# Gated linear attention and a token/channel mixer: keys of batch 0 through SP's queue, factor rows read with a step

## The chip, the cores and the metric

The kernel runs on one core of a Trainium2 chip. The metric is the device time of one execution in microseconds. The engines are named as in the profile: PE (TensorE, matmuls; PEld its weight loads), DVE (VectorE), ACT (ScalarE), POOL (GpSimd) and SP (SyncE, which only issues DMAs and waits). [...]

## The reference

Inputs are q, k, v and f_logit of 4 batches, 8 heads, 768 steps and 48 channels, and the four weights of a mixer, all float32.

```python
f = 1.0 / (1.0 + np.exp(-f_logit))
for t in range(S):
    state = f[:, :, t, :, None] * state + np.einsum('bhd,bhe->bhde', k[:, :, t], v[:, :, t])
    y[:, :, t] = np.einsum('bhd,bhde->bhe', q[:, :, t], state)
x = y.transpose(0, 2, 1, 3).reshape(B, S, H * D)          # 4 x 768 x 384
h = np.maximum(x.transpose(0, 2, 1) @ w_tok1, 0.0) @ w_tok2
u = x + h.transpose(0, 2, 1)
out = u + np.maximum(u @ w_ch1, 0.0) @ w_ch2
```

## The kernel before, in words

Each batch is cut into 6 chunks of 128 steps, with the steps on the partitions and 8 x 48 = 384 channels along the row. For a chunk, `gates` makes the logarithm of 1/f on ACT (an exponential and a logarithm, L479 and L480) and, on DVE or POOL, the low part `Llo` that the bfloat16 upper half of it leaves out (L485). `sums_and_turns` sums the logarithms along the chunk by matmuls with a triangle (L552 to L555; the last chunk of batch 0 in float32, L543), and ACT takes from PSUM the factors G and Gi = exp of minus and plus the sum (L565, L567). DVE scales q by G and k by Gi (L586); PE transposes both (L603), and DVE or ACT copies the transposes back (`qkT`, L459 and L461). `attention` multiplies them (L504), DVE masks the product (`AmT`, L640), and `rest` adds the part of earlier chunks (L671) and of this chunk (L678) to the output y, while DVE carries the state along (L649 to L654) and ACT or POOL copies it to bfloat16 (`state_bd`).

The state needs one factor a channel, that of the chunk's last step. In batch 0 it comes of small matmuls (L552) and one small exponential (`glast`, L570). In later batches ACT takes the exponential of the sums' last 32 partitions into `ends` (L574), and SP moves partition 127 of it, turned, into `glast` by a DMA (L580). `ends` lies as (parity, channel, head pair), so that this DMA reads it in a row; the sums lie as (head pair, parity, channel).

`mixer` then does the two token matmuls (L708, L724), turns u (L765), and does the two channel matmuls (L783 with a ReLU into `zT`, L802 with the final sum on DVE, L808, and the store by SP, L812). The chunks of the next batch's attention are laid between the matmuls of the mixer before it.

The order of all work is made when the program is built. Every operation is given to a planner with its engines, a rank, what it needs and makes, and an assumed duration; the planner fills each engine's queue by the earliest start, with ranks breaking ties. The table `SHIFTS` overrides rank and adds a lag for some 560 operations by number; `LATE` adds to the assumed landing of some loads. On the chip each engine runs its queue in that order and waits with semaphores. Where PE would stand idle at the start, the planner puts matmuls on a constant tile (`steady`, L849).

Loads of batch 0 go one chunk at a time. f comes by SP in float32; k, q and v come by POOL, converted to bfloat16 into `qk_sb` and `v_sb`. SP's load of f for chunk c + 2 waits for a small memset on POOL (`mark`, L382) that stands behind POOL's issue of q for chunk c, so that SP's loads are spaced by POOL's issues. Weights and later batches follow in POOL's queue. `x_nat` holds the float32 y of a batch, in three buffers; buffer 2 is first used by batch 2.

Of the kernel before, what the change touches and what calls it, by code (L numbers as in the profile page):

```python
# [86 lines left out]
)  # L87
KEPT = 3
SPLIT = 5
# [211 lines left out]
def kernel(  # L301
# [109 lines left out]
    def once(engine, fn, make, own):  # L411
        add(engine, -5.0, fn, make=make, kind=("fix", own, own))

    add(POOL, -20.0, lambda: None, kind=("load", 600, 600, 0))
    load("f", 0, 0, SP)
    load("f", 0, 1, SP)
    load("kq", 0, 0)
    mark(2)
# [7 lines left out]
    for c in range(1, NCH):  # L426
        load("kq", 0, c)
        if c + 2 < NCH:
            mark(c + 2)
            load("f", 0, c + 2, SP)  # L430
# [452 lines left out]
```

## Time and profile before

| | |
|---|---|
| median of 3 runs | 181.43 us (181.07 to 182.17) |
| profiled execution, its own time | 180.95 us |
| its span | 179.1 us |
| PE, busy | 166.3 us (93%), 11.6 us of it fillers (L849) |
| DVE, ACT, POOL, busy | 128.1, 125.8, 100.7 us |
| granted clock | 1.0 |
| SP's loads of f in batch 0, issue to landing | 4.1 us, median of 6 |
| POOL's loads of k, q and v, issue to landing | 5.3, 5.5, 5.3 us, medians of 24 |

The span is the time from the first to the last instruction of the program; the execution's own time is 1.85 us longer. Busy times of one engine overlap those of the others, so they don't add up; what counts in a stage is which engine the others wait for there.

### The profile page before, as it was taken

How to read it: one execution, taken by the hardware profiler on the slowest of the kernel's cores; microseconds unless marked ns; L12 is line 12 of the kernel's file. 1: busy time of each engine (PE TensorE's matmuls, PEld its weight loads, DVE VectorE, ACT ScalarE, POOL GpSimd, SP SyncE). 2: the span in 40 equal slices, each digit the busy share in tenths (PEclk: the TensorE clock that was granted, in tenths of full speed). 3: DMA queues.
4: the chain of work that ended last, by engine and by line, in shares of the span. 5: the costliest groups of instructions: out<-in, count | busy, mean ns of one | idle time of the engine just before them, and what ended most of it. 6: DMA issues, size and time to landing. Idle time of an engine off the chain costs nothing.

```text
span 179.1 us, 4283 instructions
## 1 busy us (share of the span) xinstructions
PE 166.3 (93%) x1649; PEld 104.8 (59%) x1653; DVE 128.1 (72%) x286; ACT 125.8 (70%) x273; POOL 100.7 (56%) x136
## 2 busy tenths in 40 slices
PE   6888898899998999799899999999999999999991
PEld 2445565556665665465566656676666666656660
DVE  6469886996878999887949987699674666501331
ACT  4678894699798786999899689976844432695000
POOL 7999569696599969977992996521102211000000
PEclk9999999999999999999999999999999999999999
DMA  7999999999999999999997999944812011200132
GB/s 105 127 165 157 148 149 182 211 142 203 183 167 152 213 247 91 199 91 89 113 161 40 89 201 137 189 91 108 93 31 89 3 44 47 90 0 0 73 117 77
DMA packets 97796, 21.54 MB, mean 120 GB/s; under 512 B 90512, under 2 KB 96912, under 8 KB 97776
## 3 DMA queue, kind: packets, MB, share of 16 engines
q0 software_dynamic: 79440, 13.77, 96.1%
q1 hardware_dynamic: 18336, 7.51, 19.0%
q8 instruction: 13, 0.21, 0.6%
q14 instruction: 7, 0.06, 0.1%
HBM read 25.17 MB, written 4.72 MB: 167 GB/s over the span
## 4 chain that ended last, share of the span: by engine, by line
PE 46%; ACT 11%; DVE 3%; issue 1%
PE ps L802 19%; PE ps L783 15%; ACT ends L574 3%; PE ps L724 2%; PE ps L708 2%; ACT zT L468 2%; PE ps L765 1%; ACT u_bf L459 1%; ACT GG L567 1%; PE ps L504 1%; PE ps L678 1%; PE ps L671 1%; PE ps L603 1%; ACT f_sb L479 1%; ACT state_bd L459 1%
## 5 line engine op out<-in xcount | busy, mean ns | idle before, releaser
L783 PE MATMUL ps<-uT,w_ch 128*128 128x384 bf16 x288 | 51.9, 326 | 1.2 <-ACT zT L468 0.7
L802 PE MATMUL ps<-w_ch,zT 128*128 128x384 bf16 (+2 forms) x300 | 52.4, 320 | 0.0
L468 ACT ACTIVATE zT<-ps 128x384 bf16<-128x384 f32 x70 | 33.2, 491 | 12.2 <-PE ps L783 9.9
L783 PEld LDWEIGHTS <-w_ch 128*128 128x128 bf16 x288 | 27.2, 98 | 18.1 <-issue 1.6
L802 PEld LDWEIGHTS <-zT 128*128 128x128 bf16 x300 | 27.7, 98 | 16.6
L640 DVE TENSOR_TENSOR AmT<-ps,tri_bf 128x512 bf16<-128x512 f32 x46 | 29.9, 683 | 3.3 <-PE ps L504 3.1
L401 POOL DMA_DIRECT2D v_sb<-in_v_dram x24 | 22.4, 931 | 4.7 <-DMA w_ch<-in_moe_w_ch_dram 4.7
L808 DVE TENSOR_TENSOR x_nat<-x_nat,ps 128x384 f32<-128x384 f32 (+2 forms) x25 | 13.3, 535 | 15.4 <-PE ps L802 15.3
L401 POOL DMA_DIRECT2D qk_sb<-in_k_dram x24 | 22.7, 944 | 0.8 <-POOLq L867 0.8
L401 POOL DMA_DIRECT2D qk_sb<-in_q_dram x24 | 22.6, 944 | 0.0
L470 DVE TENSOR_SCALAR zT<-ps 128x384 bf16<-128x384 f32 x26 | 13.8, 551 | 8.7 <-PE ps L783 8.7
L586 DVE TENSOR_TENSOR qk<-qk_sb,GG 128x768 bf16<-128x768 bf16 (+1 forms) x30 | 14.9, 501 | 6.0 <-ACT GG L567 2.6
L463 POOL CAST state_bd<-state 48x192 bf16<-48x192 f32 x13 | 4.4, 342 | 21.8 <-DVE state L654 11.4
L401 POOL DMA_DIRECT2D f_sb<-in_f_logit_dram x18 | 16.5, 943 | 0.2
L479 ACT ACTIVATE f_sb<-f_sb 128x384 f32<-128x384 f32 x24 | 12.4, 517 | 4.9 <-DMA f_sb<-in_f_logit_dram 4.7
L603 PE MATMUL ps<-ident,qk 128*128 128x128 bf16 x144 | 11.4, 220 | 1.9 <-DVE qk L586 1.8
L849 PE MATMUL ps<-steady 128*128 128x512 bf16 x37 | 11.6, 433 | 1.6 <-DVE steady L433 1.5
L574 ACT ACTIVATE ends<-ps 32x384 f32<-32x384 f32 x15 | 12.7, 861 | 0.3
L459 ACT ACTIVATE state_bd<-state 48x192 bf16<-48x192 f32 x27 | 9.7, 360 | 4.2 <-DVE state L654 3.5
L565 ACT ACTIVATE GG<-ps 128x384 bf16<-128x384 f32 x24 | 11.6, 488 | 1.4 <-PE ps L555 1.1
L603 PEld LDWEIGHTS <-qk 128*128 128x128 bf16 x144 | 8.8, 98 | 5.8 <-DVE qk L586 4.2
L567 ACT ACTIVATE GG<-ps 128x384 bf16<-128x384 f32 x24 | 11.3, 493 | 0.5 <-PE ps L555 0.3
(75 smaller groups left out, 249.2 us busy)
## 6 DMA issues: line engine op xcount, KB each, us to landing
out_dram<-x_nat SPq DMA_DIRECT2D x23, 192.0 KB, 3.0
f_sb<-in_f_logit_dram POOLq DMA_DIRECT2D x18, 192.0 KB, 5.4
qk_sb<-in_k_dram POOLq DMA_DIRECT2D x24, 96.0 KB, 5.3
qk_sb<-in_q_dram POOLq DMA_DIRECT2D x24, 96.0 KB, 5.5
v_sb<-in_v_dram POOLq DMA_DIRECT2D x24, 96.0 KB, 5.3
f_sb<-in_f_logit_dram SPq DMA_DIRECT2D x6, 192.0 KB, 4.1
w_ch<-in_moe_w_ch_dram POOLq DMA_DIRECT2D x2, 576.0 KB, 8.6
w_ch<-in_moe_w_ch_dram POOLq DMA_DIRECT2D x1, 1152.0 KB, 10.2
```

Of the source, the lines that this page charges most:

```text
L401: lambda eng=eng, into=into, of=of: eng.dma_start(out=into, in_=of),
L459: nc.scalar.activation(out_, in_, AF.Copy, bias=0.0, scale=1.0)
L468: nc.scalar.activation(out_, in_, AF.Relu, bias=0.0, scale=1.0)
L470: nc.vector.tensor_scalar(out_, in_, 0.0, None, ALU.max)
L479: add(ACT, r, lambda: nc.scalar.activation(fb, fb, AF.Exp, bias=0.0, scale=-1.0), make=[key], kind=el)
L574: add(ACT, r, lambda: nc.scalar.activation(ends[g4][96:128, :, 0:D].rearrange("t par d hp -> t hp par d"), sview()[96:128].rearrange("t (h ...
L586: add(DVE, r, lambda n=n: nc.vector.tensor_tensor(qk[i4][:, n, :, 0:D], qk_sb[nb][:, n, :, c, :], GG[i][:, n], ALU.mult), need=[(x, nb, c) ...
L603: nc.tensor.transpose(to[:, o + hp, :], blk(src)[:, hp, :], ident)
L640: add(DVE, r, lambda half=half, made=made: nc.vector.tensor_tensor(half, made(), tb4, ALU.mult), need=["tri_bf"], make=[("AmT", i, p)], ba ...
L783: nc.tensor.matmul(banks[pm.at][:, 0:384], lhsT=w[:, kt, c0:c0 + 128], rhs=uT[:, th, :, kt, :], start=(kt == 0), stop=(kt == 2))
L802: nc.tensor.matmul(banks[pm.at][:, 0:n1 - n0], lhsT=zT[:, kt, tt * 128:(tt + 1) * 128], rhs=w_ch2[:, kt, n0:n1], start=(kt == 0), stop=(kt ...
L808: add(DVE, rank("ch2", tt), lambda un=un, pm=pm, n=n1 - n0: nc.vector.tensor_tensor(un, un, banks[pm.at][:, 0:n], ALU.add), make=[("x_nat" ...
```

## The change

- Keys of batch 0 no longer come by POOL. SP loads them in float32 into buffer 2 of `x_nat`, and DVE's scaling of k reads them from there, writing bfloat16 as before. Only k of batch 0 is concerned; q and v stay with POOL.
- The marks are no longer called. SP's queue now holds f and k of chunk 0, f and k of chunk 1, and so on, twelve loads in a row that wait for nothing. POOL's queue at the start holds q and v of each chunk in turn.
- The exponential into `ends` writes in a row and reads the sums with a step (one float32 of each of the four head pairs, 384 bytes apart); before, it read in a row and wrote with a step of 16 bytes.
- `SHIFTS` is another table and `LATE` is empty; the planner's assumed sizes of loads are others (800 for SP's, 650 for POOL's q and v of batch 0). The order of the queues differs throughout: 38 fillers on PE for 41, six state copies moved from ACT to POOL, four of `zT` from DVE to ACT. The number of PE's other matmuls is the same.

```diff
-LATE = {("f", 0, 1): 900, ("f", 0, 2): 200, ("f", 0, 3): 600, ("f", 0, 4): 700, ("f", 0, 5): 900,
...
+LATE = {}
...
+            if engine == SP and n == "k":
+                into = x_nat[2][:, c, :].rearrange("t (h d) -> t h d", d=D).unsqueeze(2)
...
-            size = 1050 if n == "f" else 760
+            size = 800 if engine == SP else 1050 if n == "f" else 650 if b == 0 else 760
...
-                kind=("load", 430 if engine == SP else 900,
+                kind=("load", 800 if engine == SP else 900,
...
     load("f", 0, 0, SP)
+    load("k", 0, 0, SP)
+    load("q", 0, 0)
     load("f", 0, 1, SP)
-    load("kq", 0, 0)
-    mark(2)
-    load("f", 0, 2, SP)
     load("v", 0, 0)
...
     for c in range(1, NCH):
-        load("kq", 0, c)
-        if c + 2 < NCH:
-            mark(c + 2)
-            load("f", 0, c + 2, SP)
+        load("k", 0, c, SP)
+        if c + 1 < NCH:
+            load("f", 0, c + 1, SP)
+        load("q", 0, c)
         load("v", 0, c)
...
-                ends[g4][96:128, :, 0:D].rearrange("t par d hp -> t hp par d"),
-                sview()[96:128].rearrange("t (hp par) d -> t hp par d", par=2), AF.Exp, bias=0.0, scale=-1.0),
+                ends[g4][96:128, :, 0:D],
+                sview()[96:128].rearrange("t (hp par) d -> t par d hp", par=2), AF.Exp, bias=0.0, scale=-1.0),
...
+        def raw(n):
+            if b == 0 and n == 1:
+                return x_nat[2][:, c, :].rearrange("t (h d) -> t h d", d=D)
+            return qk_sb[nb][:, n, :, c, :]
+
...
-                qk[i4][:, n, :, 0:D], qk_sb[nb][:, n, :, c, :], GG[i][:, n], ALU.mult),
+                qk[i4][:, n, :, 0:D], raw(n), GG[i][:, n], ALU.mult),
```

The listing of the changed program gives the start of DVE's queue, behind the first chunk's work: scaling of k of chunk 1, the two masks of chunk 0, scaling of q of chunk 1, the state of chunk 0, scaling of q and k of chunk 2, the two copies of chunk 1's transposes, and so on.

More of the change, by code (lines that the diff above doesn't have):

```diff
@@ L396, in load @@
             into = dst[i][:, :, cs, :]
+            if engine == SP and n == "k":
+                into = x_nat[2][:, c, :].rearrange("t (h d) -> t h d", d=D).unsqueeze(2)
             of = src[b].rearrange("h (c t) d -> t h c d", t=C)[:, :, cs, :]
             eng = nc.gpsimd if engine == POOL else nc.sync
-            size = 1050 if n == "f" else 760
+            size = 800 if engine == SP else 1050 if n == "f" else 650 if b == 0 else 760
             add(engine, 30.0 if b else 3.0 * c - (9.0 if engine == SP else 6.0),
                 lambda eng=eng, into=into, of=of: eng.dma_start(out=into, in_=of),
-                make=[(n, i, j) for j in range(cs.start, cs.stop)],
-                kind=("load", 430 if engine == SP else 900,
+                make=[(n, i, j) for j in range(cs.start, cs.stop)] + ([("x_nat", 2, c)] if engine == SP and n == "k" else []),
+                kind=("load", 800 if engine == SP else 900,
                       128 * H, size, 8000 if b else 20000, LATE.get((n, b, c), 0)))
@@ L586, in sums_and_turns @@
             add(DVE, r, lambda n=n: nc.vector.tensor_tensor(
-                qk[i4][:, n, :, 0:D], qk_sb[nb][:, n, :, c, :], GG[i][:, n], ALU.mult),
-                need=[(x, nb, c) for x in names] + [({"q": "G", "k": "Gi"}[x], i) for x in names],
-                make=[(x + "h", i4) for x in names], kind=("el", DM * len(names), False, 2))
+                qk[i4][:, n, :, 0:D], raw(n), GG[i][:, n], ALU.mult),
+                need=[(x, nb, c) for x in names] + ([("x_nat", 2, c)] if b == 0 and names == ["k"] else []) + [({"q": "G", "k": "Gi"}[x], i) for x in names],
+                make=[(x + "h", i4) for x in names], kind=("el", DM * len(names), False, 1 if b == 0 and names == ["k"] else 2))
         if b >= TURNED:
```

126 rows, old and new, of tables (LATE, SHIFTS) are left out of this document.

## The prediction

> **What bounds the kernel now.** I read the page's busy times and slices first, then the table of stages, then the chain of waits inside the stage where TensorE (PE) stands idle, and last the forms of instructions and the DMA packets at the start.
>
> ```profile
> PE 166.3 (93%) x1649; PEld 104.8 (59%) x1653; DVE 128.1 (72%) x286; ACT 125.8 (70%) x273; POOL 100.7 (56%) x136
> ```
>
> PE is the bound of the span (179.1 us; the profiled run took 180.95 us, so 1.85 us lie around it), but 11.6 us of its busy time are fillers of L849. Its real work, some 155 us, cannot shrink by this change: the listing of the new program has the same matmuls, with 38 fillers for 41. So time can come only from the start and from PE's idle stretches. The stages (columns: PE, PEld, DVE, ACT, POOL busy, clock, DMA) show one such stretch:
>
> ```profile
> 60.00:70.00 10.00, 10.00 (x131) 6.89 (x129) 9.88 (x22) 7.65 (x19) 8.08 (x11) 1.00 1.74 162
> 70.00:80.00 10.00, 8.31 (x71) 4.88 (x67) 9.17 (x21) 9.55 (x22) 8.74 (x11) 1.00 1.78 158
> 80.00:90.00 10.00, 8.83 (x96) 5.56 (x96) 8.12 (x17) 9.03 (x20) 8.87 (x11) 1.00 1.21 95
> 90.00:100.00 10.00, 9.74 (x108) 6.46 (x106) 7.50 (x14) 8.81 (x20) 6.43 (x8) 1.00 1.03 91
> 100.00:110.00 10.00, 9.70 (x117) 6.23 (x116) 8.61 (x19) 8.51 (x19) 10.00 (x13) 1.00 1.82 155
> ```
>
> From 70 to 110 us PE misses 1.69 + 1.17 + 0.26 + 0.30 = 3.4 us, while ACT is 85 to 95% busy. The chain of waits there runs along ACT (start, length, what):
>
> ```profile
> 72.96 1.56 ACT ends L574 x2
> ...
> 81.08 0.85 ACT ends L574
> ...
> 86.82 0.85 ACT ends L574
> ...
> 90.79 0.85 ACT ends L574
> ...
> 102.76 0.87 ACT ends L574
> ```
>
> Six of the fifteen factor rows stand on it. The forms say why they are dear:
>
> ```profile
> L574 ACT ACTIVATE ends<-ps 32x384 f32<-32x384 f32 x15 | 12.7, 861 | 0.3
> L565 ACT ACTIVATE GG<-ps 128x384 bf16<-128x384 f32 x24 | 11.6, 488 | 1.4 <-PE ps L555 1.1
> L586 DVE TENSOR_TENSOR qk<-qk_sb,GG 128x384 bf16<-128x384 bf16 x12 | 4.3, 362 | 2.3 <-ACT GG L565 1.4 <-DMA qk_sb<-in_q_dram 0.8
> L485 DVE TENSOR_TENSOR Llo<-f_sb 128x384 bf16<-128x384 f32 x6 | 3.3, 553 | 0.1
> ```
>
> The same 384 elements from PSUM cost 861 ns when written 16 bytes apart, 488 ns when written in a row. The start is bound by DMA packets and by DVE: from 15 to 25 us DVE is busy for 4.40 and 4.60 of each 5 us. Packets by queue, in the stretches 12.25 to 13 us, 5.75 to 6.25, and 18.5 to 20 (q0 is GpSimd's, q1 SP's):
>
> ```profile
> q0 software_dynamic: 427, 0.04, 100.7%
> q1 hardware_dynamic: 602, 0.11, 78.6%
> ...
> q1 hardware_dynamic: 497, 0.09, 102.9%
> q0 software_dynamic: 124, 0.01, 42.6%
> ...
> q0 software_dynamic: 2231, 0.21, 269.1%
> ```
>
> A load of one chunk is 128 x 8 = 1,024 packets. Alone, q0 moves 2231/1.5 = 1,487 a us, 0.69 us a load. When both queues work, SP's takes more than half: 803 against 569 a us in the first stretch, 994 against 248 at the strongest.
>
> **The change, part by part.** *Factor rows.* The write becomes contiguous, the read steps by 384 bytes in PSUM, four at a time. The trace has no such read. Bounds: 488 ns (the step is free on the read side, a gain of 373 ns each), 861 ns (it costs there what it costs on the write), and 1,234 ns (861 + 373, dearer still). Nearest is PE's read of f_sb's upper halves at every second bf16, 332 ns against 323 without a step (L554, L555): a step that costs almost nothing, though a far smaller one. I take 488. On the chain that is 6 x 0.373 = 2.2 us, inside the 3.4 us that PE misses; next behind ACT are DVE and GpSimd, 8.1 to 9.2 of 10 us busy, which is why I don't take the whole 3.4. So the term is -2.2, with 0 and -3.4 as its ends, +2.2 if the read is dearer.
>
> [...]
>
> *Keys of batch 0.* Six of GpSimd's issues (0.94 us each) and four marker memsets (0.09 us) go; SP gets six more loads, twelve in a row with no wait between. Nothing stands behind them on SP before the first `glast` DMA at 40 us, and the buffer (`x_nat` 2) is written again only by batch 2, so no wait comes of it. DVE scales keys from float32: bound 362 ns below (no slowdown), and 553 ns above, the nearest row with float32 and bf16 operands in SBUF. I take 553: 6 x 0.19 = 1.15 us more on DVE.
>
> When do the loads land? SP: f of chunk 0 at 3.6 us as before (issue 0.81, 2.8 to landing), k of chunk 0 in the old place of f of chunk 1, 5.0; then 1024/803 = 1.28 us each: f 6.3, 8.8, 11.4, 13.9, 16.5 for chunks 1 to 5. Before, f of chunk 5 landed at 12.56 + 6.1 = 18.7, so ACT has it no later. GpSimd: q of chunk 0 goes where k went (issue 1.32, landing 4.2 later, 5.5, at 1.3 packets a ns); at 569 a us its 1,024 packets take 1.8 instead of 0.8 us, so 6.5; then 1.8 each, q and v in turn: q of chunk 1 at 10.1, q of chunk 2 at 13.7, q of chunk 3 at 17.3; then SP is through and a load takes 0.69: q of chunk 5 at 20.1. Before, q of chunk 2 landed at 8.94 + 5.0 = 13.9 and that of chunk 5 at 16.82 + 6.4 = 23.2. So the last chunk comes 3 us sooner.
>
> That is not won, because DVE then sets the pace. In the new order the scaling of q of chunk 2 is DVE's next work from about 12.7 us (chunk 0's masks and chunk 1's scalings are done), and the copies of chunk 1's transposes stand behind it. So DVE waits to 13.7. Behind it stand, up to the last mask of chunk 5: 4 scalings of q at 0.36, 4 of k at 0.55, 7 copies at 0.42, 2 differences at 0.55, 8 masks at 0.68, 8 state steps at 0.35, one copy at 0.55, together 16.5 us; 34 records overlap by 0.08 each (two masks of 683 ns last 1.28), so 13.7 us back to back, and at 94% busy 14.6. The last mask ends at 13.7 + 14.6 = 28.3 us; now it ends at 26.80 + 1.28 = 28.1. So +0.2. Behind it PE has 6 matmuls of the first mixer stage instead of 8: 2 x 0.16 = -0.3. The start gives -0.1.
>
> *Weights* come sooner, as GpSimd issues them right behind v of chunk 5: worth nothing, since the first L783 at 34.2 us waits on `u_bf` and its copies, with its weights already there. If they were late, each us would count in full.
>
> *The new order* has the same work elsewhere; ACT hands six state copies to GpSimd and takes four more of `zT`. I cost it at 0, the cover being PE's own work between 110 and 175 us, where PE is never idle.
>
> Sum: 180.95 - 2.2 - 0.1 = 178.65 on the profiled run. The median of the runs shown is 181.43, 0.48 above it; so 179.1 as a median.
>
> **The rivals.**
>
> *A, the step costs as much on the read.* [...] Then 180.95 - 0.1 = 180.85, as a median 181.3; dearer still, 183.5.
>
> *B, SP's train starves GpSimd's queue: slower than now.* For it: 994 against 248 packets a us at 5.75 us; before, SP's loads were spaced by marks, now twelve stand back to back. Against it: 803 against 569 later, under more load. At 994 and 248, SP's train is through by 14.8 us; GpSimd's queue, at 688 packets by 4.4 us, has moved 248 x 10.4 = 2,580 more, and of the 5,120 packets up to q of chunk 2 1,850 are left, 1.25 us at 1,487; with 0.85 from last packet to landing, q of chunk 2 is there at 16.9. DVE ends at 16.9 + 14.6 = 31.5, +3.4, so 178.65 + 3.2 = 181.85, as a median 182.3. Every us that q of chunk 2 lands after 12.7 counts in full; from about 16 us the kernel is no faster than now.
>
> *C, the new order puts late work on GpSimd.* It gets 19 state copies for 13, in one queue with DMA issues that wait for older landings (L401 on `w_ch`, 4.7 us in two waits, the longest 3.3). One state copy behind such a wait holds the next chunk's output and then PE. Against it: now no state copy does. Both waits on the path: 178.65 + 4.7 = 183.35, as a median 183.8.
>
> **How the numbers follow.** A measurement of this kernel tells about 1% from no change: below 179.6 or above 183.2. Forecast 0.42, own range 177.9 (the 3.4 won) to 180.2 (q of chunk 2 a us late); A 0.14, a third of it dearer; B 0.26; C 0.18. Faster: 0.34 of the forecast and 0.03 of the others, 0.37. Slower: 0.4 of B, 0.65 of C and 0.4 of A, together 0.28. Within 1%: 0.35. The range runs from 177.2 to 184.0, which leaves out the ends of C and of A's dearer third.
>
> **What would show it.** The factor rows at some 490 ns, and less than 1.5 us of PE idle between 70 and 110 us, show the first term; at 860 A holds. DVE's wait for q of chunk 2 under 1.5 us and the last mask of chunk 5 near 28.3 us show the start; a DVE wait of 3 us or more on `in_q` shows B. Keys scaled at 550 ns show the price of float32. A GpSimd state copy on the chain of waits shows C. The forecast is wrong if the first L783 starts after 36 us, or if PE is idle for more than 3 us between 70 and 110.

## The result: slower by 8%, and the profile after

The changed kernel takes 196.08 us (median of four runs, 195.38 to 200.29) where the kernel before, run beside it, takes 181.25 (180.69 to 182.17). The ratio is 1.080, with a 95% interval of 1.074 to 1.086. The forecast was 179.1, with a range from 177.2 to 184.0: wrong in size and in sign. Some executions of these kernels are disturbed; the ratios leave them out, and where that left no ratio the text says so.

The page first: busy times, and the span in 40 slices of 4.86 us each.

```profile
PE 171.6 (88%) x1646; PEld 107.6 (55%) x1650; DVE 127.2 (65%) x283; ACT 119.2 (61%) x270; POOL 98.4 (51%) x132
...
PE   6987206998999989999999989969999999999992
...
PEclk9999855799999999999999999996999999999999
```

The span grew by 15.3 us, from 179.1 to 194.4. PE has a hole in slices five and six (19 to 29 us), and its granted clock falls there: 0.5 from 22.9 us on for 13.65 us. Slice 28 has a smaller dip, 3.41 us long, after PE waited 1.9 us for the DMA that turns q and k of a later batch. The first channel matmul (L783 before, L781 now) moved from 34.2 to 48.1 us, by 13.9 us. From there to PE's last matmul it is 141.3 us before and 142.5 us after. So nearly all of the loss is in the start.

The part that the forecast counted on came true. The stages from 70 us on (PE, PEld, DVE, ACT, POOL, clock, DMA):

```profile
70.00:80.00 10.00, 9.31 (x138) 6.57 (x136) 9.92 (x22) 8.16 (x20) 9.04 (x12) 1.00 1.67 197
80.00:90.00 10.00, 9.57 (x113) 6.19 (x111) 9.22 (x19) 8.65 (x21) 9.86 (x12) 1.00 1.63 168
90.00:100.00 10.00, 9.53 (x94) 6.36 (x94) 9.95 (x24) 9.15 (x22) 9.29 (x13) 1.00 1.42 105
100.00:110.00 10.00, 10.00 (x108) 6.50 (x107) 7.95 (x17) 8.83 (x20) 8.71 (x12) 1.00 1.38 104
```

PE misses 0.69 + 0.43 + 0.47 + 0.00 = 1.6 us where it missed 3.4. (The same work lies some 14 us later now; from 84 to 124 us PE misses 1.3.) The forms (mean ns behind the busy time) give the two prices, 484 and 581 ns:

```profile
L567 ACT ACTIVATE ends<-ps 32x384 f32<-32x384 f32 x15 | 7.3, 484 | 0.3
...
L584 DVE TENSOR_TENSOR qk<-x_nat,GG 128x384 bf16<-128x384 f32 x6 | 3.5, 581 | 0.0
```

Now the start. First PE's longest wait from 16 to 48 us, then ACT in order of time:

```profile
PE ps L601 <- DVE qk L584: 7.7, 2, 7.5
```

```profile
20.40 0.52 ACT L472 ACTIVATE f_sb<-f_sb 128x384 f32<-128x384 f32 x1 [2.62 <-DMA f_sb<-in_f_logit_dram]
20.83 0.35 ACT L452 ACTIVATE state_bd<-state 48x192 bf16<-48x192 f32 x1
21.09 0.51 ACT L473 ACTIVATE L<-f_sb 128x384 f32<-128x384 f32 x1
21.61 0.36 ACT L452 ACTIVATE state_bd<-state 48x192 bf16<-48x192 f32 x1
29.39 0.52 ACT L472 ACTIVATE f_sb<-f_sb 128x384 f32<-128x384 f32 x1 [7.42 <-DMA f_sb<-in_f_logit_dram]
29.82 0.47 ACT L558 ACTIVATE GG<-ps 128x384 bf16<-128x384 f32 x1
```

ACT waits 7.42 us for f of chunk 5. Behind that wait in ACT's queue stands the factor G of chunk 3 (L558), whose sums PE had made at 18.6 to 19.1 us; DVE's scaling waits for G, and PE's transposes (L601) wait for DVE. PE is idle for 7.48 us, from 23.3 to 30.7. The half clock covers this wait and the 5.8 us of work behind it, but it did not begin with it: the clock fell at 22.9 us, 1.2 us after the end of an earlier and shorter wait, for the logarithm of f of chunk 4:

```profile
21.65 0.18 PE L545 MATMUL ps<-ones_bf,L 128*128 128x1 bf16 x1 [2.09 <-ACT L L473]
```

In the kernel before, G of chunk 3 stands ahead of the exponential of f of chunk 5 on ACT; the new order puts it behind:

```profile
15.74 0.47 ACT L565 ACTIVATE GG<-ps 128x384 bf16<-128x384 f32 x1
...
19.38 0.51 ACT L479 ACTIVATE f_sb<-f_sb 128x384 f32<-128x384 f32 x1
```

No engine waited for a key in this start, though k of chunk 5 landed last. The waits for SP's loads are all for f, 13.7 us in four waits on ACT.

Why f of chunk 5 is late the DMA queues tell. Packets from 12 to 13 us, with both queues full of work (q0 is GpSimd's, q1 SP's):

```profile
DMA packets 950, 0.13 MB, mean 134 GB/s; under 512 B 950, under 2 KB 950, under 8 KB 950
...
q0 software_dynamic: 475, 0.05, 82.5%
q1 hardware_dynamic: 475, 0.09, 82.3%
```

and from 30 to 31 us, with the weights in q0:

```profile
DMA packets 196, 0.21 MB, mean 206 GB/s; under 512 B 69, under 2 KB 196, under 8 KB 196
...
q0 software_dynamic: 134, 0.20, 107.6%
q1 hardware_dynamic: 62, 0.01, 10.6%
```

From 12 to 13 us the queues move the same number of packets, 475 each, and together 950 a us, where q0 alone moved 1,487 before (18.5 to 20 us). At this rate a load of 1,024 packets takes 1,024/475 = 2.16 us in either queue, by estimate. This sets in at 11 us and holds for most of the time to 23 us; from 5 to 11 us the shares still changed from one us to the next, and the sum was 1,045 to 1,373 a us. From 21 us on the weights (packets of 512 and 1,536 bytes) come into q0: from 25 to 26 us q0 moves 279 packets and q1 277, from 30 to 31 us 134 and 62. SP's last loads landed at 22.8 (k of chunk 4), 29.4 (f of chunk 5) and 35.6 us (k of chunk 5), against 18.7 for the last f before.

SP's issues stretched as well; the line of k's six loads shows shortest, median and longest in ns:

```profile
L395 SPq DMA_DIRECT2D x_nat<-in_k_dram x6: 558/2390/2797, 1.3 to 18.1; - x6
```

### The profile page after: what moved, and what is told of

Its sections match the earlier page's. It is cut to its first block, busy times and chain, and to the rows that moved or that the text cites. A ratio compares the mean times of both kernels' runs of the same rounds, so it can differ in the third digit from the quotient of the medians.

```text
span 194.4 us, 4288 instructions
## 1 busy us (share of the span) xinstructions
PE 171.6 (88%) x1646; PEld 107.6 (55%) x1650; DVE 127.2 (65%) x283; ACT 119.2 (61%) x270; POOL 98.4 (51%) x132
## 4 chain that ended last, share of the span: by engine, by line
PE 47%; DMA 4%; DVE 3%; ACT 2%; issue 1%; POOL 0%; POOLq 0%
PE ps L781 18%; PE ps L800 16%; DMA qkT<-qk 4%; PE ps L706 2%; PE ps L722 2%; PE ps L497 1%; PE ps L676 1%; DVE x_nat L738 1%; PE ps L601 1%; PE ps L763 1%; PE ps L669 1%; DVE AmT L638 1%; PE ps L513 1%; PE ps L547 1%; PE ps L548 1%
## 5 line engine op out<-in xcount | busy, mean ns | idle before, releaser
L781 PE MATMUL ps<-uT,w_ch 128*128 128x384 bf16 x288 | 53.1, 334 | 0.0
L461 ACT ACTIVATE zT<-ps 128x384 bf16<-128x384 f32 x74 | 35.3, 491 | 20.8 <-PE ps L781 20.1
L781 PEld LDWEIGHTS <-w_ch 128*128 128x128 bf16 x288 | 27.9, 100 | 18.0 <-issue 1.5
L800 PEld LDWEIGHTS <-zT 128*128 128x128 bf16 x300 | 27.8, 98 | 16.5
L806 DVE TENSOR_TENSOR x_nat<-x_nat,ps 128x384 f32<-128x384 f32 (+2 forms) x25 | 13.3, 534 | 13.1 <-PE ps L800 13.1
L472 ACT ACTIVATE f_sb<-f_sb 128x384 f32<-128x384 f32 x24 | 12.3, 523 | 15.0 <-DMA f_sb<-in_f_logit_dram 14.8
L456 POOL CAST state_bd<-state 48x192 bf16<-48x192 f32 x19 | 7.1, 373 | 27.0 <-DVE state L652 19.1
L601 PE MATMUL ps<-ident,qk 128*128 128x128 bf16 x144 | 13.5, 235 | 8.1 <-DVE qk L584 8.0
L584 DVE TENSOR_TENSOR qk<-qk_sb,GG 128x768 bf16<-128x768 bf16 (+1 forms) x24 | 11.9, 503 | 11.7 <-ACT GG L558 10.3
L463 DVE TENSOR_SCALAR zT<-ps 128x384 bf16<-128x384 f32 x22 | 11.8, 553 | 9.9 <-PE ps L781 9.8
L601 PEld LDWEIGHTS <-qk 128*128 128x128 bf16 x144 | 10.2, 106 | 14.1 <-DVE qk L584 10.5
L395 POOL DMA_DIRECT2D f_sb<-in_f_logit_dram x18 | 16.5, 933 | 1.2 <-DMA qk_sb<-in_q_dram 0.7
L395 POOL DMA_DIRECT2D qk_sb<-in_k_dram x18 | 16.5, 914 | 0.2 <-issue 0.2
L847 PE MATMUL ps<-steady 128*128 128x512 bf16 x34 | 13.4, 503 | 2.0 <-DVE steady L426 1.5
L558 ACT ACTIVATE GG<-ps 128x384 bf16<-128x384 f32 x24 | 11.7, 488 | 4.4 <-PE ps L548 4.2
L497 PE MATMUL ps<-qkT 48*128 48x128 bf16 x192 | 8.7, 221 | 2.8 <-DMA qkT<-qk 1.9
L706 PE MATMUL ps<-x_bf,w_tok 128*128 128x384 bf16 x48 | 10.6, 325 | 0.0
## 6 DMA issues: line engine op xcount, KB each, us to landing
out_dram<-x_nat SPq DMA_DIRECT2D x23, 192.0 KB, 2.1
f_sb<-in_f_logit_dram POOLq DMA_DIRECT2D x18, 192.0 KB, 5.2
f_sb<-in_f_logit_dram SPq DMA_DIRECT2D x6, 192.0 KB, 7.3
x_nat<-in_k_dram SPq DMA_DIRECT2D x6, 192.0 KB, 8.8
```

Of the source, the lines that this page charges most:

```text
L395: lambda eng=eng, into=into, of=of: eng.dma_start(out=into, in_=of),
L461: nc.scalar.activation(out_, in_, AF.Relu, bias=0.0, scale=1.0)
L463: nc.vector.tensor_scalar(out_, in_, 0.0, None, ALU.max)
L472: add(ACT, r, lambda: nc.scalar.activation(fb, fb, AF.Exp, bias=0.0, scale=-1.0), make=[key], kind=el)
L584: add(DVE, r, lambda n=n: nc.vector.tensor_tensor(qk[i4][:, n, :, 0:D], raw(n), GG[i][:, n], ALU.mult), need=[(x, nb, c) for x in names] + ...
L601: nc.tensor.transpose(to[:, o + hp, :], blk(src)[:, hp, :], ident)
```

## The experiments

Times are medians; each kernel ran beside the kernel before, which took 181.2 to 181.4 us in all three groups of runs. The theory after the result: SP's twelve loads in a row and GpSimd's loads slow each other down packet by packet, the weights then starve SP's last loads, and the wait at the head of ACT's queue carries that to every engine. Rivals: the new order of the queues, the factor rows, the half clock alone, SP's slow issuing alone, or the order on ACT alone.

**The factor rows alone.** The kernel before with one edit:

```diff
-                ends[g4][96:128, :, 0:D].rearrange("t par d hp -> t hp par d"),
-                sview()[96:128].rearrange("t (hp par) d -> t hp par d", par=2), AF.Exp, bias=0.0, scale=-1.0),
+                ends[g4][96:128, :, 0:D],
+                sview()[96:128].rearrange("t (hp par) d -> t par d hp", par=2), AF.Exp, bias=0.0, scale=-1.0),
```

> The kernel before with one edit: the factor rows are read with a step and written in a row, its order and loads untouched. If these rows are what ACT's chain between 70 and 110 us pays for, they fall from 861 to about 484 ns, PE's idle time in that stretch falls from 3.4 to about 1.5 us and the time by about 2 us, ratio 0.988 to 0.992. Rival: DVE or GpSimd stand right behind ACT there; then the rows fall as well, PE stays idle for some 3 us and the time stays within 0.5 us.

179.15 us (six runs, 178.29 to 180.49), ratio 0.988 (0.985 to 0.992). A row takes 482 ns:

```profile
L574 ACT ACTIVATE ends<-ps 32x384 f32<-32x384 f32 x15 | 7.1, 482 | 0.3
```

PE misses 1.65 us between 70 and 110 us. So the first term of the forecast is right by itself, 2.2 us of 181.33, and this kernel is faster than both.

**The old loads in the new order.** The changed kernel with keys by GpSimd in bfloat16 and the marks put back, the rest of its order kept (`mark_now` is GpSimd's memset that SP's next f waits for):

```diff
-            eng = nc.gpsimd if engine == POOL else nc.sync
+            eng = nc.gpsimd if engine == POOL or n == "k" else nc.sync
...
+        send(("k", 0, c))
+        send(("q", 0, c))
+        if c + 2 < NCH:
+            mark_now(c + 2)
+            send(("f", 0, c + 2))
+        send(("v", 0, c))
```

> The changed kernel with its new order on PE, ACT and DVE, but with the loads of batch 0 as before (keys by GpSimd in bfloat16, SP's f tied to the marks). Theory of the loads: the whole loss came through late landings, so the last f lands near 19 us again, the output of chunk 5 is there at 28 to 30 us instead of 42.5, and the kernel takes 178 to 182 us. Rival, the order: the queues are laid badly whatever lands when; then it stays over 188 us.

181.75 us (180.25 to 183.35), ratio 0.994 (0.990 to 0.998). Its first channel matmul starts at 35.8 us. So the new order without the new loads is no slower than the kernel before, and the loss needs the loads. The new loads in the old order were not run. The order takes back about half of the rows' gain, (0.994 - 0.988) x 181.3 = 1.0 us; this is rough, since the two intervals overlap.

**Keys back, f still untied.** As the last one, but without marks, so that SP's six f stand in a row:

```diff
+    for c in range(NCH):
+        send(("f", 0, c))
```

> The changed kernel with keys of batch 0 back on GpSimd in bfloat16, while SP's six loads of f still wait for nothing. If the six additional loads on SP are the harm and not the missing marks, all f land by about 13 us, f of chunk 5 no longer meets the weights, and the time is 179 to 183 us. Rival: untied loads on SP are enough to starve one of the queues; then k or q of the first chunks land more than 3 us later than before and the time is over 185 us.

183.41 us (179.58 to 185.21); the runs spread too far for an interval. In the profiled one f of chunk 5 landed at 13.5 and v of chunk 5 at 22.7 us, and the first channel matmul started at 36.0. Six loads in a row on SP do no large harm; whether a us or two is lost is not settled.

**The weights held back.** The changed kernel, with GpSimd waiting for k of chunk 5 ahead of the weights' issues:

```diff
+            if name == "w_tok1":
+                nc.gpsimd.tensor_copy(seen, x_nat[2][0:1, NCH - 1, 0:1])
             nc.gpsimd.dma_start(out=dst, in_=src.rearrange("(kt p) n -> p kt n", p=128))
```

> The changed kernel with one addition: GpSimd issues the weights only when k of chunk 5 has landed (a copy of one element waits for it). Theory of the shared engines: SP's last two loads were late because they alternated, packet by packet, with GpSimd's large packets of weights; without these f of chunk 5 lands at 23 to 25 us instead of 29.4 and k of chunk 5 at 25 to 27 instead of 35.6, PE's wait of 7.5 us shrinks to 2 to 4, the clock falls for a shorter time, and the time is 185 to 190 us. Rival, SP's own issues: SP takes over 2 us for each load whatever else moves; then both land within 2 us of where they did and the time stays at 194 to 199 us.

188.8 us (187.9 to 190.49), ratio 1.042 (1.037 to 1.047): half of the loss comes back. f of chunk 5 landed at 24.7 us instead of 29.4 and k at 27.1 instead of 35.6. ACT's two longest waits now cost about the same:

```profile
20.59 0.52 ACT L477 ACTIVATE f_sb<-f_sb 128x384 f32<-128x384 f32 x1 [2.67 <-DMA f_sb<-in_f_logit_dram]
...
24.76 0.52 ACT L477 ACTIVATE f_sb<-f_sb 128x384 f32<-128x384 f32 x1 [2.60 <-DMA f_sb<-in_f_logit_dram]
```

The half clock lasted 6.83 us instead of 13.65, and the first channel matmul came at 42.4 us.

**Fillers in the long wait.** 34 more fillers (L847) on PE behind the sums of chunk 4:

```diff
+        if seen4 and not filled and op.kind[0] == "fill":
+            idle(34)
+            filled = True
```

> The changed kernel with 34 more fillers on TensorE, put into the long wait before the last chunk of batch 0, so that TensorE has work while it waits for the late loads. Loads, gates and everything else are as in the changed kernel. Theory (the late landings of f and k of chunk 5 set the end of the start, and the clock of 0.5 from 22.9 to 36.5 us is only a consequence of the 7.5 us idle stretch): the clock stays near 1.0 through the start, the first channel matmul comes only 1 to 2.5 us sooner than 48.1 us, since k of chunk 5 still lands near 35.6 us, and the time is 193.5 to 195 us. Rival (the half clock is the main loss: 13.65 us at 0.5 hold some 6.8 us of full-speed work): over 5 us come back, below 191 us.

194.65 us (191.88 to 196.22), ratio 1.065 (1.057 to 1.072). The clock was 0.5 for 3.41 us only, and the time did not fall below 191 us, as the rival asked. By itself this run does not decide: in its profile f of chunk 5 landed at 24.7 us, with the loads untouched, and the fillers went on to 32.3 and held up the transposes behind them. The trace of the changed kernel sets a firmer bound. Of its 13.65 us at half clock PE is idle for 7.48, and the other 6.17 us cost at most 3.1 us of the 14.8, half of them, by estimate: PE's transposes took 310 ns there (31 to 36 us), against 219 from 48 us on. One stretch agrees: from PE's transposes after the wait to the first channel matmul it is 17.4 us in the changed kernel (30.75 to 48.15) and 14.8 here (32.14 to 46.94), and part of these 2.6 us is work that DVE had done ahead here. So the half clock alone is not the loss.

**The last f behind the gates on ACT.** The exponential and the logarithm of f of chunk 5 go behind G and Gi of chunks 3 and 4:

```diff
+            if is_sums(op, 5):
+                for x in late:
+                    x.fn()
```

> The changed kernel with the exponential and the logarithm of f of chunk 5 moved on ScalarE to just ahead of chunk 5's own sums, behind the gates of chunks 3 and 4, which in the changed kernel stand behind ScalarE's 7.4 us wait for that f. Loads are untouched. Landing theory (k and f of chunk 5 land at 35.6 and 29.4 us whatever ScalarE does in between): chunks 3 and 4 go on from about 19.5 us and TensorE's idle stretch is broken up, but chunk 5 still ends when k of chunk 5 lets it; saved at most 2 us, about 194 us. Rival (the wait at the head of ScalarE's queue is itself the loss): the whole idle stretch of 7.5 us goes, about 189 us.

195.19 us (191.46 to 198.44), ratio 1.063 (1.055 to 1.071). The masks of chunk 3 were done at 30.6 us, 6.8 us sooner than in the changed kernel (37.3), and the long idle stretch is broken up. But f of chunk 5 landed only at 33.2 and k at 36.5 us. PE waited 4.5 us for that f's logarithm, because in PE's queue the sums of chunk 5 (L537 here) stand ahead of the attention of chunk 4; the last mask ended at 41.3 us. The landings set the end, as the theory says, but through f: DVE's last scalings waited for G of chunk 5 (36.1 us), not for the key. From 28 to 32 us the equal counts show at their plainest, 475 packets against 476, with 0.72 MB against 0.09 MB:

```profile
q0 software_dynamic: 475, 0.72, 95.0%
q1 hardware_dynamic: 476, 0.09, 20.4%
```

**SP's loads first, alone.** GpSimd's loads of q and v wait until k of chunk 5 has landed:

```diff
+    for c in range(NCH):
+        send(("f", 0, c))
+        send(("k", 0, c))
...
+    nc.gpsimd.tensor_copy(seen, x_nat[2][0:1, NCH - 1, 0:1])
+    for c in range(NCH):
+        send(("q", 0, c))
+        send(("v", 0, c))
```

> The changed kernel with all twelve q and v loads of GpSimd's queue held until k of chunk 5, the last of SP's twelve float32 loads, has landed; the two constant matrices are made ahead of that. So SP's queue has the DMA engines to itself, and then GpSimd's has. Sharing theory (the two queues take turns packet by packet and together move fewer packets than either alone): SP's loads take about 0.9 to 1.0 us each, issues stay under 1.2 us, k of chunk 5 lands by 14.5 us; GpSimd's then run at some 1,490 packets a us, v of chunk 5 lands at 24 to 25 us; about 183 us, faster than the changed kernel by over 10 us although every q and v starts later. Rival (SP's issuing itself is slow, 2 to 2.8 us a load whatever the other queue does): k of chunk 5 lands at 25 us or later, v of chunk 5 at 35 us or later, 195 us or more.

192.0 us (191.66 to 192.62), ratio 1.060 (1.057 to 1.063). The landings are as sharing wants them, k of chunk 5 at 14.2 us. The queue from 4 to 14 us, and SP's issues of k:

```profile
q1 hardware_dynamic: 10367, 1.96, 99.8%
```

```profile
L397 SPq DMA_DIRECT2D x_nat<-in_k_dram x6: 558/930/1305, 1.3 to 10.5; - x6
```

Alone, q1 moves 1,037 packets a us and an issue takes 0.93 us, against 475 and 2.39 in the changed kernel. So SP is not slow by itself; its issues are long when the other queue is full too. The 183 us of the expectation were wrong for another reason: GpSimd issues a load each 0.88 us, so v of chunk 5 came at 28.7 and not at 24 to 25, and the masks of six chunks take 16.5 us from the first to the last (22.98 to 39.50; before, 11.69 to 28.09). Here the late first chunk was not made good.

**Three of the six keys on SP.** Keys of chunks 3 to 5 go back to GpSimd:

```diff
+            if engine == SP and n == "k" and c < 3:
+                into = x_nat[2][:, c, :].rearrange("t (h d) -> t h d", d=D).unsqueeze(2)
...
+            eng = nc.gpsimd if engine == POOL or (n == "k" and c >= 3) else nc.sync
```

> The changed kernel with only the keys of chunks 0 to 2 by SP in float32; those of chunks 3 to 5 come by GpSimd in bf16 as in the kernel before. SP issues nine loads (six f, three keys) in a row, GpSimd fifteen. Sharing theory (the queues take turns packet by packet only as long as both hold packets; after that GpSimd's queue alone moves some 1,490 a us): f of chunk 5, now ninth on SP, lands where the ninth load landed in the changed kernel, near 20.4 us; nine of GpSimd's fifteen are through by then, the other six take 4 to 5 us, so v of chunk 5 lands near 25 us, before any weights; the clock stays at 1.0, the last mask of chunk 5 ends at 30 to 31.5 us, and the time is 182 to 184.5 us: half the keys cost almost nothing. Rival (every load moved to SP costs its share): half way between the kernel with all keys on GpSimd and the changed one, 189 to 190 us.

184.62 us (184.01 to 185.31), ratio 1.018 (1.015 to 1.022), 0.1 above the theory's range and 4 below the rival's. f of chunk 5 landed at 21.5 us (20.4 expected) and v at 24.9 (25 expected). The last mask ended at 33.3, later than expected: ACT still waited 1.76 us for that f with G of chunk 3 behind it, and PE's wait of 1.9 us was followed by 3.41 us of half clock. The first three keys cost 1.2 us over the kernel with all keys on GpSimd (183.4, which has no interval), the last three 11.5. This fits a loss that lies in what is still in SP's queue when the weights come.

**Both remedies.** The weights wait for k of chunk 4, and the last f stands behind the gates on ACT:

```diff
+                nc.gpsimd.tensor_copy(seen, x_nat[2][0:1, NCH - 2, 0:1])
...
+            if is_sums(op, 5):
+                for x in late:
+                    x.fn()
```

> The changed kernel with two edits together: GpSimd's issues of the four weight loads wait until k of chunk 4 has landed (so that no large packets share the engines with SP's last loads), and ScalarE's exponential and logarithm of f of chunk 5 stand behind the gates of chunks 3 and 4. All twelve loads of f and k stay on SP. Theory (two causes one behind the other: the weights' packets starve SP's last two loads, and f of chunk 5 at the head of ScalarE's queue holds back chunks whose data is there): f of chunk 5 lands near 25 us and k near 28 us, the masks of chunks 3 and 4 are done by 30 us, the last mask of chunk 5 ends at 32.5 to 34 us, the first channel matmul comes at 38.5 to 40 us, and the time is 186 to 188.5 us. What is left over the kernel with all keys on GpSimd, 3 to 5 us, is the slower rate of two deep queues. Rival (the order on ScalarE is worth nothing, as it was by itself): as with the weights held alone, 188.8 us, with the last mask at 36 us or later.

189.66 us (188.64 to 191.06), ratio 1.047 (1.041 to 1.053): a miss. f and k of chunk 5 landed at 24.9 and 26.8 us as expected, and chunk 3 had its masks by 28.6. But in its new place the exponential of that f started 3.5 us after its landing, behind a copy of y:

```profile
27.95 0.49 ACT L458 ACTIVATE x_nat<-ps 128x384 f32<-128x384 f32 x1
28.34 0.51 ACT L478 ACTIVATE f_sb<-f_sb 128x384 f32<-128x384 f32 x1
```

PE's sums of chunk 5 waited for it to 29.5, and behind them the attention of chunk 4 to 31.1, so that chunk 4's masks ended at 32.9 (30 expected) and the last at 34.7 (32.5 to 34). The profiled run also had 6.83 us of half clock from 11.5 us on, after a wait of 1.8 us. By time this order is worth nothing over the weights held alone. By the profile the start is 1.9 us shorter (first channel matmul at 40.5 us), and the rest 2.0 us longer, with a half clock of 3.41 us in it at 124 us. Whether the other runs are alike is left open.

## Why the prediction was wrong

The start in one table, in us from the span's start. ACT's start on f of chunk 5, the last mask and the first channel matmul:

| kernel | f of chunk 5 on ACT | last mask ends | first channel matmul | span |
|---|---|---|---|---|
| before | 19.4 | 28.1 | 34.2 | 179.1 |
| old loads, new order | 19.5 | 30.0 | 35.8 | 178.4 |
| keys back, f untied | 19.5 | 30.3 | 36.0 | 180.6 |
| three keys on SP | 21.5 | 33.3 | 39.1 | 183.2 |
| weights held | 24.8 | 36.7 | 42.4 | 186.7 |
| changed | 29.4 | 42.4 | 48.1 | 194.4 |

In the new order, all rows but the first, the last mask ends 10.5 to 13 us after ACT starts on that f, the first channel matmul comes 5.8 us later, and the rest takes 143 to 146 us. In the last three rows ACT starts on that f as it lands, after waits of 1.76, 2.60 and 7.42 us. There the landing of one 1,024-packet load sets the start. The first two rows have that f at the same time, and in the old order, with G of chunk 3 ahead of it, the last mask ends some 2 us sooner.

Landings differ between executions. With the changed kernel's loads untouched f of chunk 5 landed at 29.4 us (changed), 24.7 (fillers) and 33.2 (ACT's order) in three profiles, with the weights held back at 24.7 and 24.9 in two. So one profile does not price the weights. The times do: 187.9 to 190.49 us over four runs with the weights held, 195.38 or more in the changed kernel, and 191.46 or more in the other two.

**Factor rows, -2.2 us: right.** 484 ns where 488 was taken; PE's idle time from 70 to 110 us is 1.6 us, at the edge of the 1.5 given; 2.2 us of time when tried alone. Rival A had the stepped read lose the 373 ns again; with reads 384 bytes apart in PSUM the instruction took 484 ns. Rival A falls.

**Keys in float32: nearly right.** 581 ns each on average where 553 was taken, 0.17 us over six; the median is 554, and one took 712.

**The landings: the step that failed.** The prediction gave SP 1.28 us a load and f of chunk 5 at 16.5 us. It took 803 against 569 packets a us, a stretch of the kernel before in which SP's queue held a load now and then and its issues were spaced by the marks, and carried that over to twelve loads in a row. With both queues full, from 11 us on, it is 475 against 475, or 2.16 us a load. f of chunk 2 still landed at 10.0, for 8.8 forecast, and six more loads at 2.16 make 23.0 us for f of chunk 5; with the weights held it was 24.7. The prediction also had the sum of the queues stay near 1,370 a us; it fell to 950.

**"Weights come sooner: worth nothing": wrong by some 7 us.** They were asked only whether they come too late, never what they share the engines with. Their issues began 5 us sooner (13.4 us against 18.6), and they landed no sooner (29.0 to 36.6 us against 25.4 to 35.1). Holding them back brought 196.1 to 188.8.

**"ACT has it no later": the wait behind it was not followed.** The step looked at q of chunk 2 and at DVE. That load landed at 13.1 us, close to the 13.7 forecast, and DVE's pace from there was not the limit. What stood behind f of chunk 5 on ACT, the factor of chunk 3, was never named, though the order of the queues could be read beforehand.

**Rival B had the wrong victim.** It had SP's loads starve GpSimd's queue by 994 to 248. That rate was there, at 7 to 8 us (1,042 to 181), and gone by 11 us. SP's own queue came last, behind GpSimd's large packets. **Rival C** did not come: no state copy on GpSimd held the start. **The new order** was costed at 0 and took about 1.0 us, by intervals that overlap. In seven of the nine profiles of the new order PE waits 1.7 to 2.0 us, near 120 to 131 us, for the DMA that turns q and k, and in two of them 3.41 us of half clock followed (before and with the rows alone it waits 0.8 us at most); that this is the 1.0 us was not tried.

Of the 14.8 us (196.08 - 181.25), then: about 7.3 are the weights' packets. At most 3.1 us are half clock, partly the same microseconds. About 5.4 us (188.8 against 183.4) come of the six more loads on SP: the slower rate of two full queues (475 packets a us each), with ACT's order handing it on. How this part divides is open: with f moved back on ACT it was PE's queue that held chunk 4 behind the same f. The last 2.1 us, from 183.4 to 181.3, are not settled; they and the size of the 5.4 hang on the kernel whose runs spread. The rows' gain is in all of these kernels but the first: against the rows alone (179.15) the new loads and the new order lose 16.9 us.

## What to carry to other kernels

Here, moving loads to a second queue did not make the DMA engines move more packets: with both queues full they moved 950 a us, where q0 alone had moved 1,487. Take the rate from a stretch in which both queues are as full as they will be, and count all that is then still in them, the large transfers too. A load that comes "sooner" can compete with small loads that are not through yet: holding the weights back took the time here from 196.08 to 188.8 us. And for each load that comes later, read what stands behind its first use on that engine: here one load of f held two chunks whose own f had long been there, on ACT and again on PE.

## What the runs showed of the hardware

- Two full queues of small packets (96 and 192 bytes) moved 950 packets a us together where each moved 475 (changed, 12 to 13 us); q0 alone moved 1,487 in the kernel before (18.5 to 20 us), and q1 alone 1,037 with SP's loads first (4 to 14 us). In these stretches a packet of q1 took 28 ns in company and 15 to 16 alone.
- SP's issues took 0.93 us (median of six) with its queue alone and 2.39 for the same six loads with both queues full.
- Half clock came in pieces of 3.41, 6.83 or 13.65 us, whole multiples of 3.41; a piece that sets in at the end of the program (at 193.5 us in the changed kernel, behind PE's last matmul) is left out. In the five starts with one piece of it (changed, weights held, fillers, three keys, both remedies) it began between 0.1 us before and 1.2 us after the end of a PE wait of 1.8 to 2.6 us. Not every such wait was followed by one: with f moved on ACT a wait of 2.1 us at 12 us was not. Nor does the clock's row show every slow stretch: with SP's loads first PE was idle for 10.3 us, its transposes then took 311 ns, as against 220 in the kernel before at a clock of 1.00 and 310 in the changed kernel at 0.50, and the row still says 1.00.
